# Two transformer layers on one core: the second layer's queries, keys and values with two token blocks sharing one pass of 64 + 64 inner rows

## The chip, the cores and the metric

The kernel runs on one core of a Trainium2 chip. The metric is the time of one execution in microseconds (us) on the device. Five engines work side by side: TensorE (PE in the profile; its weight loads are PEld), VectorE (DVE), ScalarE (ACT), GpSimd (POOL) and SyncE (SP), which here only issues transfers. TensorE writes its sums into banks of PSUM; the other engines take them out from there.

## The reference

Two equal layers over 2048 tokens of 576 features. Each is a sliding, dilated attention (32 heads of 18 features, 8 keys at distances 0, 2, .. 14) and a feed-forward part with SiLU, both on the normalized input, both added to it.

```python
def _A_ref(x, wqkv, wo):
    qkv = (x @ wqkv).reshape(B, S, 3, H, Dh).transpose(2, 0, 3, 1, 4)
    q, k, v = qkv[0], qkv[1], qkv[2]
    idx = pos[:, None] - (jnp.arange(8) * 2)[None, :]
    ...
    attn = _softmax(jnp.where(mask, logits, -1e9) * ...)
    return einsum("bhsw,bhswd->bhsd", attn, vg).reshape(B, S, D) @ wo

def _B_ref(x, w1, w2):
    return _silu(x @ w1) @ w2

for _ in range(2):
    x = x + _A_ref(_layernorm(x), A_wqkv, A_wo)
    x = x + _B_ref(_layernorm(x), B_w1, B_w2)
```

The change concerns `x @ wqkv` of the second layer alone: 576 inner features, 1728 columns.

## The kernel before

**Numbers.** Inputs are float32. A factor is split into two half-precision parts, high and low, and a product is made as high x high + high x low + low x high. For `x @ wqkv`, `passes` (a generator) lists the passes of TensorE: for each of the four full slices of 128 features three passes, and for the last 64 features two. Those two use a fifth slice of the input in which rows 0 to 63 hold the high parts of the 64 features and rows 64 to 127 their low parts. Slice 4 of the weights holds the high parts twice, slice 9 the low parts twice, so the first pass gives (high + low) x high, and the second (high + low) x low. That makes 14 passes of 128 rows and 128 tokens by 432 columns for a block.

**Tiles and stages.** The tokens are cut into four chunks of 512, a chunk into four blocks `j` of 128. A stage `s` from 0 to 7 is one chunk in one layer, so the second layer has the stages 4 to 7, and its first chunk is the fifth stage. The attention works in four units `u` of 8 heads; a unit's weights give 144 queries, keys and values each, 432 columns. In the second layer `attention` makes, for every stage, unit and block, one operation of 14 passes (`qkv_matmul`, line 726) into a bank of tag `zq`, and ScalarE takes it out into `kvs` and `qts` (lines 794 and 796). Then VectorE makes the products with the keys, the softmax and the sums over the values (lines 828 to 869).

The input's parts come from `layer_norm`: statistics (548), a Newton iteration for the reciprocal root (521 to 530), the normalized row (574), then the two halves (`halves`, 579, and `halves_lo`, 483), which go through a transposing transfer into tile `xa`. For the stages 6 and 7 the halves are made earlier, at the end of stages 2 and 3 (tile `xn`, `keep`), and loaded back.

The feed-forward part of the stages from 2 on (`ffn_pairs`) forms seven combinations of the input (`forms`, lines 1139 to 1182, tiles `yo`, `yh`, then `xb`) and multiplies each with a combination of the weights: a product is seven passes of 256 columns (line 1209). VectorE and ScalarE add them up (1213, 1216), apply SiLU, and split the result into the parts of `h` (1244, 1247), from which the second product is made, 12 passes of 288 columns at a time (line 1326). A pair of feature blocks `q` takes three banks in turn (tag `zz`).

**What sets the order.** Nothing is ordered by hand. Every operation is recorded with an engine, a duration that somebody wrote down, the tiles it reads and writes, and a priority; `Plan.order` plays the work through with these numbers and starts on each engine the ready operation of lowest priority number for which the tile slots are free. The order that comes out is the program. The tags `zz` and `zq` stand for the same four banks, so an operation that wants a bank competes with the feed-forward products. Attention operations of the second layer have priorities 3.0 to 3.4 on TensorE (`AT`), the feed-forward part of stage 3 has 3.5 and above, that of stage 4 has 4.5 and above: the second layer's attention is interleaved with the feed-forward work of the stages before it.

`S.slots("z", ...)`, `"misc"`, `"zz"` and `"zq"` all name the banks `z0`, `z1`, `misc0`, `misc1`; in the profile a product into one of them reads `z` or `misc`.

Of the kernel before, what the change touches and what calls it, by code (L numbers as in the profile page):

```python
# [14 lines left out]
ALU = mybir.AluOpType  # L15
AX = mybir.AxisListType

P = 128
D = 576
# [6 lines left out]
NC = 4  # L26
NJ = 4
# [248 lines left out]
def sliding_attention_silu_ffn(ctx: ExitStack, tc: tile.TileContext, x, wqkv, wo, w1, w2, out):  # L276
# [209 lines left out]

    def transposed(src, dst, key, j, prio, on_pe=False):


        if on_pe:  # L490
            m = Buf("acc")

            def turn():
                t = fl(T(m).bitcast(F16))
                for k in range(9):
                    nc.tensor.transpose(t[:, k * P:(k + 1) * P], T(src)[:, k, :], ident)
            op("PE", 0.5, turn, [(src, 0), (src, 1)], [m], prio)
            return op("ACT", 1.05, lambda: nc.scalar.activation(  # L498
                dst(), fl(T(m).bitcast(F16))[:, 0:9 * P].rearrange("p (a b) -> p a b", a=9), AF.Copy), [m], [(key, j)], prio - 9)
        return op("SP", 1.34, lambda: nc.sync.dma_start_transpose(dst(), fl(T(src))), [(src, 0), (src, 1)], [(key, j)], prio,  # L500
                  nbytes=P * 9 * P * 4)
# [32 lines left out]
    def layer_norm(xs, prio, into, on_act, on_pe=False, late=(), own=False, keep=None):  # L534
# [33 lines left out]
        for j in range(NJ):  # L568
# [8 lines left out]
            def halves(y=y, yh=yh):  # L577
                f = fl(T(yh))
                nc.vector.tensor_scalar(f[:, 0:D], T(y), 1.0, None, op0=ALU.mult)
                halves_lo(T(y), f, 1.0)  # L580
# [8 lines left out]
            else:  # L589
                op("DVE", 0.52, norm, [xs[j], (mv, j), (nt, "r", j)], [y] if keep else [y, (xT, "hold")], prio, after=late)  # L590
                o = op("DVE", 1.23, halves, [y], [(yh, 0), (yh, 1)], prio)
# [135 lines left out]

    def stage(g):
        t = T(g)
        return t[:, :QR] if g.tag == "hs" else fl(t.bitcast(F32))[:, :QR]  # L730
# [26 lines left out]
    def attention(s, xT, wq, more=None):  # L757
# [4 lines left out]
        for u in range(NU):  # L762
# [12 lines left out]
            else:  # L775
# [6 lines left out]
                else:  # L782
# [5 lines left out]
                    op("SP", 0.8, edge, [("eds", lay, par, u)], [(kv, "edge")], pr_, nbytes=20000, lanes=2, after=free)  # L788
                for j in range(NJ):
                    m = Buf("zq" if lay else "misc")  # L790
# [6 lines left out]
                    for a, b in ((0, 6), (6, 12), (12, 14)) if s + u + j == 0 else ((0, 14),):  # L797
                        op("PE", 2.56 * (b - a) / 14, lambda j=j, m=m, w=w, a=a, b=b: qkv_matmul(xT, w, j, m, a, b),
                           [(xT, j)] + [w.keys[5 * h + k] for k in range(a // 3, (b + 2) // 3) for h in range(2)],
                           [m, (kv, "hold")] if lay else [m], pr_, after=free)  # L800
# [672 lines left out]
    def norm(s):  # L1473
# [14 lines left out]
        normed[s] = layer_norm(xs, p, "xa", False, late=late, own=True)  # L1488
# [23 lines left out]
    for s in range(NL * NC):  # L1512
# [10 lines left out]
        if 2 <= s < NC:  # L1523
            layer_norm(X[s], AN[s + NC] + 0.0, None, False, own=True, keep=xn[s - 2])
# [46 lines left out]
```

## Time and profile before

| | us |
|---|---|
| median of 3 runs | 2135.34 (2133.32 to 2140.86) |
| the profiled execution | 2134.51 |
| its span in the profile | 2132.7 |
| TensorE's second-layer queries, keys, values | from 894 to 1497 of the span |

The profile is one execution. Its page gives each engine's busy time, and the trace behind it can be asked for a timeline, for the busy time in a stretch, and for one line of the program. In a timeline a row merges neighbours of one kind: `x14` is fourteen passes, the second column is the time from the start of the first to the end of the last. A pass's own duration includes the time to run through the array, so that passes overlap; the time that a pass takes up is the distance between two starts. A bracket at a row's end is idle time of the engine before it and what ended it.

### The profile page before, as it was taken

Reading aid. Unit: us, or ns where it says so; the run is one execution under the profiler, and the core shown is the slowest. Engines: PE = TensorE matmul, PEld = TensorE weight load, DVE = VectorE, ACT = ScalarE, POOL = GpSimd, SP = SyncE. Lnnn points to the kernel's source line nnn. Section 1 sums busy time; section 2 is a strip of 40 time slices with the busy share of each in tenths; the row PEclk is TensorE's granted clock in tenths of the full one; section 3 lists DMA queues with packets and bytes.
Section 4 is the critical chain, followed back from the end, with each engine's and each line's share of the span. In section 5 each row is a group of like instructions: output and inputs, shape, how many; then the busy total and the mean of one; then the engine's idle time right before and its main releaser. Section 6 shows DMA issues by size and latency. Waiting matters only on the chain.

```text
span 2132.7 us, 41915 instructions
## 1 busy us (share of the span) xinstructions
PE 2093.9 (98%) x16017; PEld 1554.6 (73%) x16017; DVE 1811.8 (85%) x2909; ACT 1025.3 (48%) x1857; POOL 388.7 (18%) x628
## 2 busy tenths in 40 slices
PE   9999899999999999999999999999999999999998
PEld 5556466656666788877777777777788888888887
DVE  8999999999977899789989998998997748666665
ACT  7555787644335455243424433333444444444442
POOL 2223656242232241011101010000000000000000
PEclk9999999999999999999999999999999999999999
DMA  6586777597889988795768996776999998779772
GB/s 183 155 228 247 246 261 249 189 258 254 253 170 283 302 248 255 169 263 169 211 179 211 227 300 187 192 194 192 262 302 308 335 262 227 225 208 274 214 209 69
DMA packets 377633, 489.08 MB, mean 229 GB/s; under 512 B 150600, under 2 KB 300724, under 8 KB 373080
## 3 DMA queue, kind: packets, MB, share of 16 engines
q1 hardware_dynamic: 332456, 336.85, 56.2%
q0 software_dynamic: 42960, 148.45, 21.6%
q8 instruction: 125, 2.05, 0.4%
q10 hardware_dynamic: 2016, 1.11, 0.2%
q14 instruction: 76, 0.62, 0.1%
HBM read 350.96 MB, written 86.85 MB: 205 GB/s over the span
## 4 chain that ended last, share of the span: by engine, by line
PE 62%; DMA 7%; DVE 5%; issue 3%; POOL 0%; ACT 0%; SPq 0%; DVEq 0%; POOLq 0%; ACTq 0%
PE acc L1326 17%; PE z L1209 12%; PE misc L1209 11%; PE acc L1299 9%; PE z L726 3%; PE acc L904 3%; PE misc L726 3%; PE acc L1387 3%; PE z L1368 2%; DMA w<-wfs 2%; DMA w<-w2s 1%; DMA wq<-in_B_w_dram 1%; DMA xb<-yo 1%; DVE prs L828 1%; DVE lg L832 1%
## 5 line engine op out<-in xcount | busy, mean ns | idle before, releaser
L1209 PEld LDWEIGHTS <-w 128*128 128x128 f16 x5292 | 516.7, 98 | 82.4 <-issue 8.9
L1326 PE MATMUL acc<-w,h 128*128 128x288 f16 x3456 | 448.7, 287 | 1.4 <-DVE h L1247 0.9
L1326 PEld LDWEIGHTS <-h 128*128 128x128 f16 x3456 | 338.3, 98 | 86.4 <-DVE h L1247 1.8
L1209 PE MATMUL z<-xb,w 128*128 128x256 f16 x2695 | 341.7, 273 | 3.9 <-DVE wq L1216 1.9
L1209 PE MATMUL misc<-xb,w 128*128 128x256 f16 x2597 | 331.5, 273 | 5.4 <-DMA w<-wfs 3.0
L1387 PE MATMUL acc<-w,h 128*128 128x288 f16 x1728 | 215.4, 286 | 1.1 <-DMA w<-w2s 1.1
L726 PEld LDWEIGHTS <-xa 128*128 128x128 f16 x1344 | 130.8, 98 | 111.9 <-issue 1.9
L1387 PEld LDWEIGHTS <-h 128*128 128x128 f16 x1728 | 168.3, 98 | 45.6 <-issue 1.5
L861 DVE TENSOR_TENSOR prs<-kvs,pe 128x1152 f32<-128x1152 f32 x128 | 169.8, 1350 | 0.8
L828 DVE TENSOR_TENSOR prs<-qts,kvs 128x2304 f32<-128x2304 f32 x64 | 163.3, 2552 | 5.4 <-DMA kvs<-kvs 2.8
L832 DVE TENSOR_REDUCE lg<-prs 128x128 f32<-128x2304 f32 x64 | 162.9, 2545 | 0.8
L915 DVE SCALAR_TENSOR_TENSOR x<-acc,d,x 128x576 f32<-128x576 f32 x136 | 110.1, 811 | 41.8 <-PE acc L1326 35.2
L1368 PE MATMUL z<-xb,w 128*128 128x512 f16 x588 | 130.9, 383 | 7.9 <-ACT h L1370 4.0
L868 DVE TENSOR_TENSOR prs<-prs 128x1152 f32<-128x1152 f32 (+1 forms) x128 | 135.0, 1055 | 3.3
L1308 DVE SCALAR_TENSOR_TENSOR x<-acc,d2x,x 128x576 f32<-128x576 f32 (+1 forms) x85 | 68.8, 810 | 68.5 <-PE acc L1299 68.4
L726 PE MATMUL z<-wq,xa 128*128 128x432 f16 x658 | 125.2, 346 | 0.0
L904 PE MATMUL acc<-wos,yo 128*128 128x288 f16 x896 | 113.7, 286 | 3.0 <-DMA yo<-yh 1.8
L1368 PEld LDWEIGHTS <-w 128*128 128x128 f16 x588 | 57.6, 98 | 78.1 <-issue 6.5
L1299 PEld LDWEIGHTS <-h 128*128 128x128 f16 x924 | 90.2, 98 | 24.0 <-DVE h L1271 2.6
L904 PEld LDWEIGHTS <-yo 128*128 128x128 f16 x896 | 87.4, 98 | 27.1 <-DMA yo<-yh 2.3
L726 PE MATMUL misc<-wq,xa 128*128 128x432 f16 x518 | 100.1, 346 | 2.7 <-ACT xa L498 1.3
L1368 PE MATMUL z<-xb,wq 128*128 128x512 f16 x420 | 94.5, 384 | 2.6 <-ACT h L1370 2.6
(300 smaller groups left out, 3158.9 us busy)
## 6 DMA issues: line engine op xcount, KB each, us to landing
w<-wfs SPq DMA_DIRECT2D x756, 160.0 KB, 3.9
w<-w2s SPq DMA_DIRECT2D x180, 288.0 KB, 4.8
wq<-wqs SPq DMA_DIRECT2D x17, 1080.0 KB, 6.1
kvs<-kd POOLq DMA_DIRECT2D x8, 1584.0 KB, 8.2
kvs<-wts SPq DMA_DIRECT2D x81, 144.0 KB, 2.7
w<-w1s SPq DMA_DIRECT2D x36, 320.0 KB, 9.2
wfs<-xa POOLq DMA_DIRECT2D x18, 640.0 KB, 4.9
w2s<-w POOLq DMA_DIRECT2D x36, 288.0 KB, 4.2
```

Of the source, the lines that this page charges most:

```text
L726: nc.tensor.matmul(T(m)[:, :3 * UC], a, b, start=n == 0, stop=n == len(pl) - 1)
L828: nc.vector.tensor_tensor(T(pr), T(qt)[:, j:j + 2, None, :].to_broadcast([P, 2, W, UC]), win(T(kv), j, 2), op=ALU.mult)
L832: nc.vector.tensor_reduce(T(lg)[:, j:j + 2].rearrange("p a w h -> p (a w h)"), T(pr).rearrange("p a w (h d) -> p (a w h) d", d=DH), axis=A ...
L861: nc.vector.tensor_tensor(T(pr)[:, a].rearrange("p w (h d) -> p w h d", d=DH), v, T(pe)[:, j + a, :, :, None].to_broadcast([P, W, UH, DH]) ...
L868: nc.vector.tensor_tensor(t[:, :, 0:h, :], t[:, :, 0:h, :], t[:, :, h:2 * h, :], op=ALU.add)
L904: nc.tensor.matmul(T(acc)[:, h, 0:288], a, b[:, h * 288:(h + 1) * 288], start=n == 0, stop=n == len(pl) - 1)
L915: nc.vector.scalar_tensor_tensor(t, acc[:, :, 0:288], d, t, op0=ALU.mult, op1=ALU.add)
L1209: nc.tensor.matmul(t, w[:, u, :], v[:, r, :], start=first and m == 0, stop=m == 6, skip_group_check=True)
L1299: nc.tensor.matmul(T(acc)[:, j, 0:KH], T(hb[t])[:, a, row[k], j * P:(j + 1) * P], T(wb[k, t])[:, w, :], start=k in (5, 1, 2) and t == 0 an ...
L1326: nc.tensor.matmul(T(acc)[:, h, 0:288], T(hb[t])[:, a, f, j * P:(j + 1) * P], T(wbs[t][f])[:, h, w, :], start=t == 0 and f == 0 and m == 0 ...
L1368: nc.tensor.matmul(T(z), v, u, start=m == 0, stop=m == len(pl) - 1)
L1387: nc.tensor.matmul(T(acc)[:, h, 0:288], T(hb[q])[:, a, j * P:(j + 1) * P], T(wbs[q][0])[:, h, w, :], start=q == 0 and m == 0, stop=q == n ...
```

## The change

Two blocks `j` and `j + 1` of a unit make a pair. Each keeps the first 13 of its 14 passes. The fourteenth, (high + low) x low, is reduced to high x low over 64 rows: the even block's on rows 0 to 63, the odd block's on rows 64 to 127, as two instructions of 64 rows each that write to different banks. (The term low x low of these 64 features is thereby left out.) For the odd block the high parts have to lie in rows 64 to 127, so its last slice holds the halves in swapped order, which the new `halves_turned` writes; the weights' slice 9 holds the low parts in both halves already, and for the 13 other passes the order of the two halves does not matter, since slice 4 of the weights holds the same rows twice.

The recorded operations are still one for each block. The even block's has its 13 passes and both half passes; it now takes both banks of the pair and reads both blocks of `xa`. The odd block's has 13 passes. Their written durations are 2.56 and 2.38, where both had 2.56.

```diff
+    def halves_turned(src, f):
+        nc.vector.tensor_scalar(f[:, 0:512], src[:, 0:512], 1.0, None, op0=ALU.mult)
+        nc.vector.tensor_scalar(f[:, D:D + 64], src[:, 512:D], 1.0, None, op0=ALU.mult)
+        for o, a, b, h in ((640, 0, 512, 0), (512, 512, D, D)):
+            nc.vector.scalar_tensor_tensor(f[:, o:o + b - a], src[:, a:b], 1.0, f[:, h:h + b - a],
+                                           op0=ALU.mult, op1=ALU.subtract)
...
-            def halves(y=y, yh=yh):
+            def halves(j=j, y=y, yh=yh):
                 f = fl(T(yh))
+                if swap and j % 2:
+                    halves_turned(T(y), f)
+                    return
                 nc.vector.tensor_scalar(f[:, 0:D], T(y), 1.0, None, op0=ALU.mult)
                 halves_lo(T(y), f, 1.0)
...
-                o = op("DVE", 1.23, halves, [y], [(yh, 0), (yh, 1)], prio)
+                o = op("DVE", 1.38 if swap and j % 2 else 1.23, halves, [y], [(yh, 0), (yh, 1)], prio)
...
+    def qkv_pair(xT, w, j, a, b, second):
+        xk = lambda i: lambda k: T(xT)[:, k, (j + i) * P:(j + i + 1) * P]
+        if second:
+            pl = list(passes(xk(1), w))[:13]
+            for n, (u, v) in enumerate(pl):
+                nc.tensor.matmul(T(b)[:, :3 * UC], u, v, start=False, stop=n == len(pl) - 1)
+            return
+        for n, (u, v) in enumerate(list(passes(xk(0), w))[:13]):
+            nc.tensor.matmul(T(a)[:, :3 * UC], u, v, start=n == 0, stop=False)
+        for i, m in ((0, a), (1, b)):
+            r = slice(64 * i, 64 * i + 64)
+            nc.tensor.matmul(T(m)[:, :3 * UC], xk(i)(4)[r], w(9)[r], start=i == 1, stop=i == 0)
...
+                pairs = [Buf("zq") for _ in range(NJ)] if lay else []
                 for j in range(NJ):
-                    m = Buf("zq" if lay else "misc")
+                    m = pairs[j] if lay else Buf("misc")
...
+                    if lay:
+                        op("PE", 2.56 if j % 2 == 0 else 2.38, lambda j=j, w=w, pairs=pairs: qkv_pair(
+                            xT, w, j - j % 2, *pairs[j - j % 2:j - j % 2 + 2], j % 2),
+                           [(xT, i) for i in ((j, j + 1) if j % 2 == 0 else (j,))] + w.keys,
+                           [m, pairs[j + 1], (kv, "hold")] if j % 2 == 0 else [m], pr_, after=free)
-                    for a, b in ((0, 6), (6, 12), (12, 14)) if s + u + j == 0 else ((0, 14),):
+                    for a, b in () if lay else ((0, 6), (6, 12), (12, 14)) if s + u + j == 0 else ((0, 14),):
...
-        normed[s] = layer_norm(xs, p, "xa", False, late=late, own=True)
+        normed[s] = layer_norm(xs, p, "xa", False, late=late, own=True, swap=True)
...
-            layer_norm(X[s], AN[s + NC] + 0.0, None, False, own=True, keep=xn[s - 2])
+            layer_norm(X[s], AN[s + NC] + 0.0, None, False, own=True, keep=xn[s - 2], swap=True)
```

Since the order is worked out from durations and free slots, it changes from the fifth stage's second unit to the end of the second layer's attention. Two places show what moved.

The first is on TensorE, the third block of the seventh stage's first unit. Before, its last passes into one bank stand ahead of the last group of second products (`w`, `h`) of the fourth stage:

```order
L726 LDWEIGHTS xa
L726 MATMUL misc_96<-wq,xa 128x432
L726 LDWEIGHTS xa
L726 MATMUL misc_96<-wq,xa 128x432
L1326 LDWEIGHTS h
L1326 MATMUL acc_99<-w_87,h 128x288
L1326 LDWEIGHTS h
L1326 MATMUL acc_99<-w_87,h 128x288
```

Now the same block ends in the two half passes (line 749), the second into the partner's bank, and the partner's 13 passes (line 743) follow at once:

```order
L746 LDWEIGHTS xa
L746 MATMUL z_94<-wq,xa 128x432
L749 LDWEIGHTS xa
L749 MATMUL z_94<-wq,xa 128x432
L749 LDWEIGHTS xa
L749 MATMUL misc_96<-wq,xa 128x432
L743 LDWEIGHTS xa
L743 MATMUL misc_96<-wq,xa 128x432
L743 LDWEIGHTS xa
L743 MATMUL misc_96<-wq,xa 128x432
```

Behind the partner's last pass stands the fifth stage's feed-forward part (products of `xb` and `w`):

```order
L743 LDWEIGHTS xa
L743 MATMUL misc_96<-wq,xa 128x432
L1238 LDWEIGHTS w_70
L1238 MATMUL z_95<-xb,w_70 128x256
L1238 LDWEIGHTS w_70
L1238 MATMUL z_95<-xb,w_70 128x256
```

The block has moved from ahead of the last second products of the fourth stage to behind the first two groups of second products of the fifth; its partner has hardly moved. Ahead of those groups two products of seven passes have come in its stead.

The second place is on VectorE, ahead of its first write of `h` in the fifth stage (line 1247, now 1276). `x_75` and `x_76` are the halves of the fourth stage's chunk, which is normalized here for the eighth stage. Before:

```order
L1216 TENSOR_TENSOR wq<-misc_97,wq 128x256
L574 TENSOR_SCALAR x_75<-x_75,mv_91,nt_92 128x576
L579 TENSOR_SCALAR yh<-x_75 128x576
L483 SCALAR_TENSOR_TENSOR yh<-x_75,yh 128x512
L483 SCALAR_TENSOR_TENSOR yh<-x_75,yh 128x64
L1216 TENSOR_TENSOR wq<-misc_96,wq 128x256
L1216 TENSOR_TENSOR wq<-z_95,wq 128x256
L574 TENSOR_SCALAR x_75<-x_75,mv_91,nt_92 128x576
L1247 SCALAR_TENSOR_TENSOR h<-h,sh_304 128x1024
L574 TENSOR_SCALAR x_76<-x_76,mv_91,nt_92 128x576 x2
```

and now:

```order
L1245 TENSOR_TENSOR wq<-misc_96,wq 128x256
L1245 TENSOR_TENSOR wq<-z_95,wq 128x256
L861 TENSOR_REDUCE lg_80<-prs 128x128
L488 TENSOR_SCALAR yh<-x_75 128x512
L489 TENSOR_SCALAR yh<-x_75 128x64
L491 SCALAR_TENSOR_TENSOR yh<-x_75,yh 128x512
L491 SCALAR_TENSOR_TENSOR yh<-x_75,yh 128x64
L869 TENSOR_TENSOR lg_80<-lg_80,mrow 128x256
L870 TENSOR_REDUCE mx_83<-lg_80 128x32
L871 TENSOR_TENSOR lg_80<-lg_80,mx_83 128x256
L1276 SCALAR_TENSOR_TENSOR h<-h,sh_304 128x1024
```

The odd block's halves (488 to 491) and both norms of `x_76` have come ahead of that write. The attention's product, sum and first softmax step (861 to 871 here) stood ahead of it before too, only further up; no row that stood ahead stands behind now.

More of the change, by code (lines that the diff above doesn't have):

```diff
@@ L532, in newton, with layer_norm @@
             nc.vector.tensor_scalar(T(nt)[:, 2, js], T(mv)[:, js, 0], -1.0, None, op0=ALU.mult)
-    def layer_norm(xs, prio, into, on_act, on_pe=False, late=(), own=False, keep=None):
+    def layer_norm(xs, prio, into, on_act, on_pe=False, late=(), own=False, keep=None, swap=False):
         st, mv, nt, xT = Buf("st"), Buf("mv"), Buf("nt"), Buf(into) if into else None
@@ L796, in evac @@
                         nc.scalar.activation(T(qt)[:, j, :], T(m)[:, 0:UC], AF.Copy, scale=d)
-                    for a, b in ((0, 6), (6, 12), (12, 14)) if s + u + j == 0 else ((0, 14),):
+                    if lay:
[4 more added lines that the diff above has]
+                    for a, b in () if lay else ((0, 6), (6, 12), (12, 14)) if s + u + j == 0 else ((0, 14),):
                         op("PE", 2.56 * (b - a) / 14, lambda j=j, m=m, w=w, a=a, b=b: qkv_matmul(xT, w, j, m, a, b),
                            [(xT, j)] + [w.keys[5 * h + k] for k in range(a // 3, (b + 2) // 3) for h in range(2)],
-                           [m, (kv, "hold")] if lay else [m], pr_, after=free)
+                           [m], pr_, after=free)
                     op("ACT", 0.78, evac, [m, ("su", u)], [(kv, j), (qt, j)], pr_ - (0 if s else 9))
```

## The prediction

> **What bounds the kernel now.** I read the head of the page first, then the engines' busy time in the stretch in which the second layer's queries, keys and values are made, then the timelines of TensorE and VectorE at one place in it.
>
> ```profile
> span 2132.7 us, 41915 instructions
> PE 2093.9 (98%) x16017; PEld 1554.6 (73%) x16017; DVE 1811.8 (85%) x2909; ACT 1025.3 (48%) x1857; POOL 388.7 (18%) x628
> 900.00:1500.00 600.00, 595.55 (x4599) 448.91 (x4598) 542.53 (x767) 238.71 (x467) 66.86 (x113) 1.00 0.77 210
> 894.00:1497.00 603.00, 168.12 (x896) 87.54 (x896) 1.00 0.77 209
> ```
>
> The third row gives, from 900 to 1500 us, the busy time of PE, PEld, DVE, ACT and POOL, then granted clock, DMA share and GB/s; the fourth is PE and PEld for line 726 alone. PE is busy for 595.55 of 600 us at full clock, so work taken off PE is worth its full length unless PE then waits for something else. That something is near: DVE is busy for 542.53 of the same 600. The 896 passes of line 726 are 64 blocks of 14: the change makes 32 pairs of them.
>
> The place to watch is the seam at which TensorE goes from the fourth chunk's feed-forward part to the fifth's, whose inputs VectorE has to make first. PE there (start, length, what, and in brackets the idle time before it):
>
> ```profile
> 1200.11 2.72 PE L726 MATMUL z<-wq,xa 128*128 128x432 f16 x14
> 1202.66 1.63 PE L1326 MATMUL acc<-w,h 128*128 128x288 f16 x12
> ...
> 1209.39 2.73 PE L726 MATMUL misc<-wq,xa 128*128 128x432 f16 x14
> 1211.95 1.27 PE L1326 MATMUL acc<-w,h 128*128 128x288 f16 x9
> ...
> 1220.78 0.93 PE L1209 MATMUL z<-xb,w 128*128 128x256 f16 x7
> 1221.54 0.93 PE L1209 MATMUL misc<-xb,w 128*128 128x256 f16 x7
> ...
> 1224.54 0.92 PE L1209 MATMUL z<-xb,w 128*128 128x256 f16 x7 [0.28 <-DVE h L1216]
> ...
> 1231.44 0.93 PE L1209 MATMUL z<-xb,w 128*128 128x256 f16 x7 [1.22 <-DVE wq L1216]
> 1232.20 0.65 PE L1326 MATMUL acc<-w,h 128*128 128x288 f16 x4
> 1233.12 2.62 PE L1326 MATMUL acc<-w,h 128*128 128x288 f16 x20 [0.27 <-DVE h L1247]
> 1235.58 2.72 PE L726 MATMUL z<-wq,xa 128*128 128x432 f16 x14
> ```
>
> The reader is to see three things. A block of 14 passes takes 2.55 us from its start to that of the next work (1200.11 to 1202.66): 182 ns a pass. A product of seven takes 0.76 us (1220.78 to 1221.54). And each wait at the seam names DVE. VectorE at the same place:
>
> ```profile
> 1216.30:1239.40 23.10, 22.02 (x56) 1.00 1.07 306
> 1216.37 0.43 DVE L1177 TENSOR_TENSOR yo<-wos,yo 128x256 f16<-128x256 f32 x1 [3.04 <-ACT yo L1172]
> ...
> 1228.79 0.57 DVE L574 TENSOR_SCALAR x<-x,mv,nt 128x576 f32<-128x576 f32 x1
> 1229.40 0.46 DVE L579 TENSOR_SCALAR yh<-x 128x576 f16<-128x576 f32 x1
> 1229.89 0.83 DVE L483 SCALAR_TENSOR_TENSOR yh<-x,yh 128x512 f16<-128x512 f32 x2
> ...
> 1231.79 1.28 DVE L1247 SCALAR_TENSOR_TENSOR h<-h,sh 128x1024 f16<-128x1024 f32 x1
> 1232.98 1.06 DVE L574 TENSOR_SCALAR x<-x,mv,nt 128x576 f32<-128x576 f32 x2
> ```
>
> DVE is busy for 22.02 of 23.10 us (first row), and at 1231.79 it writes the h for which PE waits at 1233.12. Here DVE sets the time, and PE only has to be there.
>
> **The change part by part.** *The passes.* A pair had 28 passes and now has 26 full ones and two of 64 rows. Side by side the two cost one pass, so 182 ns a pair are saved: 32 x 0.182 = 5.8 us, of which 17 pairs (3.1 us) stand ahead of the product at 1221.54 and 15 (2.7 us) behind. The trace has no pass of fewer than 128 rows (all read 128\*128), so the price is bounded from both sides:
>
> ```profile
> L726 PE MATMUL z<-wq,xa x658: 343/346/347, 151.3 to 1492.0; 128*128 128x432 f16 x165
> L726 PEld LDWEIGHTS <-xa x1344: 95/98/100, 17.1 to 1494.3; 128*128 128x128 f16 x192
> ```
>
> Below: 182 ns saved a pair. Above: if the array has to run empty before and after, each of two passages costs what a pass lasts beyond its slot, 346 - 182 = 164 ns, so 2 x 164 - 182 = 146 ns are lost a pair, and with two weight loads of 98 ns uncovered 342 ns. I take the saving: the nearest rows are the changes from 432 to 288 or 256 columns above, with another operand on either side, and they follow one another without a gap.
>
> *A rule to weigh.* After those rows: the Trainium skill, page "TensorEngine Tiling (Array Packing)", section Tiling Modes, states that a change of the tiling mode drains TensorE; its page "TensorE: Matmul & The Clock Gate", Part 3, has passes in separate row groups start about 4 ns apart. By the first alone the pair's sum would be nearer the upper bound, by the second it is the lower; no run here yet shows either.
>
> *The moved block.* The third block of the seventh chunk's first unit (1209.39 above) stood ahead of the seam. As it now needs two of the four banks at once, it stands behind the fifth chunk's first two groups of line 1326, next to its partner (1235.58). So PE comes to the product at 1221.54, for which it has the same work ahead otherwise, 2.55 + 3.1 = 5.6 us earlier. Work that stood ahead of the group at 1232.20 and is now behind it: 2.55 us, less two products of 0.76 us that went the other way: **+1.0 us**.
>
> *VectorE.* An odd block's halves take four instructions instead of three; the added one has 64 columns, and the copy loses 64 of 576.
>
> ```profile
> L483 DVE SCALAR_TENSOR_TENSOR yh<-x,yh 128x64 f16<-128x64 f32 x12 | 2.6, 218 | 0.0
> ```
>
> At most 0.22 us, less 64/576 of 0.46 us: 0.17 us a block, eight blocks. Seven are hidden in the 57 us that DVE is idle between 900 and 1500. At the seam the order matters more: ahead of that h stand two norms more (1.06 us, row 1232.98) and an odd block's halves (0.46 + 0.83 + 0.17 = 1.46 us), and nothing that stood ahead has left: **+2.5 us**. From below, the wait of 3.04 us at 1216.37 could swallow all of it, so 0; from above, a wait of that size more, 5.5 us. I take 2.5, since the added rows stand behind the place of that wait. Behind this h are queued the softmax and the next values of the attention, and PE's group at 1232.20.
>
> So the wait at the seam grows by 2.5 us (h later) and by 5.6 - 2 x 0.76 = 4.1 us (PE earlier): 6.6 us. The 5.8 us saved are more than spent, though part of that wait is the moved block's own time, which PE still does behind it.
>
> *The clock.* A wait can cost more than its length:
>
> ```profile
> 719.62 0.94 PE L1209 MATMUL z<-xb,w 128*128 128x256 f16 x7 [0.60 <-DMA w<-wfs]
> 722.25 1.33 PE L1209 MATMUL misc<-xb,w 128*128 128x256 f16 x7 [1.69 <-DMA w<-wfs]
> 722.80:726.20 3.40, 3.40 (x17) 0.52 0.96 299
> ```
>
> After 2.3 us of waiting the clock was 0.52 for 3.4 us, some 1.6 us lost. At 1222 to 1233 it stayed at 1.00 with waits spread out. Bounds 0 and 1.6; I take half, **+0.8 us**.
>
> *At nothing:* the banks (the second is taken 2.4 us sooner; three others turn meanwhile, and if they didn't, a wait as at 1231.44, 1.22 us, is the price); the even block's wait for its partner's transposed block (made well before, except for the first pair); weight loads that change places on SP, where PE waited this much from 900 to 1850:
>
> ```profile
> PE misc L1209 <- DMA w<-wfs: 1.3, 2, 0.8
> ```
>
> Their price, if the cover goes, is another 1.3 us. The few stores that swap neighbours on POOL release nothing PE waits for soon.
>
> *Sum*, from the group at 1232.20 on, since what happens before it ends in the wait: +2.5 + 1.0 - 2.7 + 0.8 = +1.6 us. The profiled execution took 2134.51 us (span and 1.8 us around it): 2136.1. The median shown, 2135.34, lies 0.83 above it: **2137 us**.
>
> **The rivals.**
> *The saving passes through.* If VectorE makes the seam's inputs as early as PE now comes, all 5.8 us remain: 2129.5. For it: PE's own waits at the seam are short now. Against it: 22.02 of 23.10 us, and more DVE work ahead, not less.
> *The halves don't run side by side* (the change doesn't do what it says): 28 slots as before, and only the order is left: 2.5 + 1.0 = +3.5, with little clock loss 2139.
> *The array runs empty at each change of rows*, the case on the slower side. Place: both sides of each pair's half passes; price 146 ns a pair. The 17 pairs ahead (2.5 us) fill the time that the moved block left, so the wait hides them; behind come 15 x 0.146 = 2.2: 2.5 + 1.0 + 2.2 = +5.7, 2141. With the loads uncovered, 342 ns, the 17 pairs (5.8 us) exceed the 2.55 us by 3.3, which then replaces the 2.5: 3.3 + 1.0 + 15 x 0.342 = +9.4, 2144.7. It is slower by over 0.3% from 3.5 + 15c = 6.4, c = 0.19 us a pair. The Trainium skill's rule on draining ("TensorEngine Tiling (Array Packing)", Tiling Modes) would lead to this case.
>
> **How the numbers follow.** A difference under 0.3% (6.4 us) is about what a measurement of this kernel can't tell from no change. Chances: my sum 0.42, passing through 0.10, no side by side 0.15, running empty 0.33, of which 0.13 with c above 0.19. Faster by over 0.3% needs more than the whole saving, below 2128.9: 0.03. Slower, above 2141.7: 0.13. Within: 0.84. The range goes from the saving passing through nearly whole, 2130, to running empty with half of the loads uncovered, 2143.
>
> **What would show it.** The two half passes' starts lie a few ns apart (right) or 182 ns (no side by side); the gap from the last full pass to the first half, and from the second half to the next full pass, is 182 ns, or near 346 (running empty). The group that stood at 1232.20 waits for DVE's h, and PE's waits at the seam add up to some 8 us instead of the 1.8 in the brackets above. If those waits stay as they are, the seam was judged wrongly; if new waits of over 2 us appear elsewhere, the order was.

## The result and the profile after

| | median of the runs, us | span of the profiled execution, us |
|---|---|---|
| before | 2135.38 (2133.32 to 2140.86, 7 runs) | 2132.7 |
| after | 2147.51 (2139.32 to 2150.63, 7 runs) | 2148.9 |

After against before is 1.005 (95%: 1.0033 to 1.0066): some 12 us slower by the medians, 7 to 14 by the interval, outside the forecast range of 2130 to 2143. Three executions, two of the kernel before at 4473 and 5892 us and one with two shared passes at 9103 us, were in a slow state and are left out here and below. The profiled execution of the changed kernel is the slowest of its seven runs, 16.1 us above that of before.

The head of its page, engines' busy time:

```profile
span 2148.9 us, 41911 instructions
PE 2098.4 (98%) x16017; PEld 1551.2 (72%) x16017; DVE 1814.0 (84%) x2917; ACT 1025.5 (48%) x1857; POOL 388.3 (18%) x628
```

PE is busy for 4.5 us more, and the span grew by 16.2: most of it is waiting. The half passes first, by line (count, then min/median/max of the duration in ns), and then one pair on the timelines of PE and of its weight loads:

```profile
L749 PEld LDWEIGHTS <-xa x64: 91/93/93, 900.7 to 1502.8; 64*128 64x128 f16 x64
L749 PE MATMUL misc<-wq,xa x32: 352/353/354, 900.7 to 1502.8; 64*128 64x432 f16 x32
```

```profile
1143.72 2.54 PE L746 MATMUL misc<-wq,xa 128*128 128x432 f16 x13
1146.19 0.36 PE L749 MATMUL misc<-wq,xa 64*128 64x432 f16 x2
1146.47 2.55 PE L743 MATMUL misc<-wq,xa 128*128 128x432 f16 x13
1148.86 1.44 PE L746 MATMUL z<-wq,xa 128*128 128x432 f16 x7
```

```profile
1146.18 0.10 PEld L749 LDWEIGHTS <-xa 64*128 64x128 f16 x2 [0.36 <-issue]
1146.47 2.12 PEld L743 LDWEIGHTS <-xa 128*128 128x128 f16 x13 [0.19 <-issue]
```

Both half passes of a pair together span 0.36 us, one alone lasts 0.353: they run side by side, 3 ns apart in their starts. But thirteen passes at 182 ns would bring the half passes at 1146.09, and they start at 1146.19; and the next full pass comes 0.28 us behind them instead of 0.18. Over all 32 pairs the last full pass and the first half pass start 278 ns apart, the second half pass and the next full pass 285, and the full pass after that follows 194 ns later instead of 182. A pair takes 5.14 us (1143.72 to 1148.86); 28 full passes take 5.11 (1143.94 to 1149.05 in the kernel with the order alone, below).

Within a block a weight load starts 2 ns after the pass before its own. Here the load of the half pass starts at 1146.183 us, 275 ns after the last full pass (1145.908) and 93 ns after that pass's slot is over; the load of the next full pass is late in the same way. A load takes 91 to 99 ns, about what each change costs.

PE at the seam, to be laid beside the rows of before in the prediction:

```profile
1205.75 2.61 PE L1355 MATMUL acc<-w,h 128*128 128x288 f16 x20
1208.20 2.54 PE L746 MATMUL z<-wq,xa 128*128 128x432 f16 x13
...
1213.34 6.04 PE L1355 MATMUL acc<-w,h 128*128 128x288 f16 x48
1219.22 0.93 PE L1238 MATMUL z<-xb,w 128*128 128x256 f16 x7
1219.98 0.93 PE L1238 MATMUL misc<-xb,w 128*128 128x256 f16 x7
1224.67 1.68 PE L1238 MATMUL z<-xb,w 128*128 128x256 f16 x7 [3.77 <-DMA xb<-yo]
1226.14 1.70 PE L1238 MATMUL misc<-xb,w 128*128 128x256 f16 x7
...
1233.79 0.92 PE L1238 MATMUL z<-xb,w 128*128 128x256 f16 x7 [0.26 <-DVE wq L1245]
...
1238.76 0.66 PE L1355 MATMUL acc<-w,h 128*128 128x288 f16 x4 [0.98 <-ACT h L1273]
1240.75 1.15 PE L1355 MATMUL acc<-w,h 128*128 128x288 f16 x8 [1.33 <-DVE h L1276]
...
1245.90 0.27 PE L1238 MATMUL misc<-xb,w 128*128 128x256 f16 x1 [0.95 <-DVE wq L1245]
```

The brackets add up to 7.29 us. Behind the first wait seven passes take 1.47 us (1224.67 to 1226.14) instead of 0.76: half the clock, for 35 passes. Then VectorE, in the two stretches up to the first write of `h` (its start ends the second stretch; the columns are length, busy time and number, granted clock, DMA share, GB/s), of before:

```profile
900.00:1195.00 295.00, 267.33 (x398) 1.00 0.75 206
1195.00:1231.79 36.79, 32.87 (x69) 1.00 1.04 252
```

and of after:

```profile
900.00:1195.00 295.00, 261.33 (x394) 1.00 0.73 200
1195.00:1239.41 44.41, 41.61 (x81) 0.92 1.05 292
```

`h` comes 7.62 us later. Of this 2.74 us are more work (302.94 against 300.20) and 4.88 are more idle time (36.47 against 31.59): 6.00 more ahead of 1195, of which 1.12 are made up behind. The largest waits of VectorE for PE between 900 and 1195 (us in total, how many, the longest), of before:

```profile
DVE x L915 <- PE acc L1326: 6.9, 6, 1.8
DVE o L915 <- PE acc L904: 2.9, 1, 2.9
```

and of after:

```profile
DVE x L944 <- PE acc L1355: 7.4, 9, 1.6
DVE o L944 <- PE acc L933: 4.4, 1, 4.4
```

With the smaller ones, the waits for PE there grew from 11.7 to 16.0 us and those for ScalarE from 2.8 to 4.8.

Where PE loses is worked out by counting columns: the time at which the same number of columns has been issued in one execution and in that of before. The changed kernel is 1.9 us late at 1215, 8.8 at 1260, 10.8 at 1500, 12.7 at 1565, 15.8 at 1765 and 16.1 at the end. The same kernel again, the first of the experiments, has 1.9, 9.6, 10.4, 11.1, 12.0 and 11.6: the 7 to 8 us at the seam are always there, while the 2 and 3 us of 1540 and 1770 vary from execution to execution.

### The profile page after: what moved, and what is told of

It is laid out like the page before. It is cut to its first block, busy times and chain, and to the rows that moved or that the text cites. A ratio compares the mean times of both kernels' runs of the same rounds, so it can differ in the third digit from the quotient of the medians.

```text
span 2148.9 us, 41911 instructions
## 1 busy us (share of the span) xinstructions
PE 2098.4 (98%) x16017; PEld 1551.2 (72%) x16017; DVE 1814.0 (84%) x2917; ACT 1025.5 (48%) x1857; POOL 388.3 (18%) x628
## 4 chain that ended last, share of the span: by engine, by line
PE 80%; DMA 9%; DVE 7%; issue 2%; ACT 1%; SPq 1%; POOL 0%; DVEq 0%; ACTq 0%; POOLq 0%
PE acc L1355 18%; PE z L1238 12%; PE misc L1238 11%; PE acc L1328 8%; PE z L1397 7%; PE acc L1416 7%; PE z L736 5%; PE acc L933 5%; PE misc L743 2%; PE z L743 2%; PE misc L746 2%; PE z L746 2%; DMA wq<-in_B_w_dram 1%; DMA w<-w2s 1%; DMA xb<-yh 1%
## 5 line engine op out<-in xcount | busy, mean ns | idle before, releaser
L1399 ACT ACTIVATE h<-z,d 128x512 f32<-128x512 f32 x72 | 49.1, 682 | 83.9 <-PE z L1397 80.7
L1242 ACT ACTIVATE wq<-misc 128x256 f32<-128x256 f32 x97 | 36.8, 380 | 94.9 <-PE misc L1238 94.9
L1328 PE MATMUL acc<-kvs,h 128*128 128x288 f16 x498 | 76.2, 286 | 0.4 <-DVE h L1300 0.4
```

The costliest lines, as they stand in the source:

```text
L1328: nc.tensor.matmul(T(acc)[:, j, 0:KH], T(hb[t])[:, a, row[k], j * P:(j + 1) * P], T(wb[k, t])[:, w, :], start=k in (5, 1, 2) and t == 0 an ...
```

## The experiments

Each was timed against the kernel before on the same chip. "Late" is PE's lateness by columns, as above.

### Order or half passes

> The changed kernel unaltered, for a second profile beside the others on one chip. Theory A (the two half passes start together but each change between 128 and 64 rows costs some 98 ns, so a pair takes 19 ns more than 28 full passes, and the loss is the new order's waits): some 10 us over the kernel before, with the wait at the seam near 1225 us of the same size again (3.8 us, and a half clock after it), and the waits near 945, 957, 1550 and 1780 us only if they belong to the order. Theory B (the pairs themselves cost the time, by waits inside them): the same total, but the pairs' gaps differ from those of the first profile.

2147.72 (2144.16 to 2151.53), ratio 1.0053 (1.0037 to 1.0070).

The new order with 28 full passes a pair:

```diff
-        for n, (u, v) in enumerate(list(passes(xk(0), w))[:13]):
-            nc.tensor.matmul(T(a)[:, :3 * UC], u, v, start=n == 0, stop=False)
-        for i, m in ((0, a), (1, b)):
-            r = slice(64 * i, 64 * i + 64)
-            nc.tensor.matmul(T(m)[:, :3 * UC], xk(i)(4)[r], w(9)[r], start=i == 1, stop=i == 0)
+        pl = list(passes(lambda k: T(xT)[:, k, (j + i) * P:(j + i + 1) * P], w))
+        for n, (u, v) in enumerate(pl):
+            nc.tensor.matmul(T(m)[:, :3 * UC], u, v, start=n == 0, stop=n == len(pl) - 1)
```

> The changed kernel's order, banks and swapped halves with 14 full passes of 128 rows in every block (28 a pair, no half pass). Theory A: as the changed kernel, 0.6 us less of passes, so some 9 to 10 us over the kernel before, and the same wait at the seam near 1225 us. Theory B: the loss goes with the half passes, so within 3 us of the kernel before.

2145.87 (2142.74 to 2151.97), ratio 1.0045 (1.0028 to 1.0062); 7.8 us lost at the seam. And the half passes in the order of before, in the 22 pairs that stand together there (these blocks have the swapped halves too):

> The kernel before with its own order; swapped halves for the odd blocks, and 22 of the 32 pairs (those whose odd block follows the even one directly on TensorE) with the two half passes, put at the start of the odd block's passes; the other 10 pairs keep 28 full passes. Theory A: 22 x 0.019 = +0.4 us and little else, so within 2 us of the kernel before. Theory B: 22/32 of the loss, some +8 us. If the half passes saved what they were meant to, 22 x 0.182 = -4.0 us.

2135.68 (2132.07 to 2140.41), ratio 0.9998 (0.9987 to 1.0010). The order alone carries the loss; the half passes alone neither save nor cost, to within 3 us.

### The price of a change of rows

A full pass between the two half passes, so four changes a pair:

```diff
-            nc.tensor.matmul(T(m)[:, :3 * UC], xk(i)(4)[r], w(9)[r], start=i == 1, stop=i == 0)
+            nc.tensor.matmul(T(m)[:, :3 * UC], xk(i)(4)[r], w(9)[r], start=i == 1, stop=False)
+            if i == 0:
+                u, v = pl[12]
+                nc.tensor.matmul(T(a)[:, :3 * UC], u, v, start=False, stop=True)
```

> The changed kernel with the even block's last full pass put between the two half passes: four changes of rows a pair instead of two, and the halves no longer together. Theory A: 2 x 98 + 182 - 3 = 375 ns a pair more, 32 x 0.375 = +12 us over the changed kernel, less what falls into the seam's wait (17 pairs ahead of it): +6 to +12 us. If the price is not one of the change but of the pair as such, +182 ns a pair, +3 to +6 us.

2157.80 (2156.34 to 2160.16), ratio 1.0101 (1.0084 to 1.0118): 10 us above the changed kernel. Over the 64 changes in either direction the starts are 278 or 289 ns apart on the way to 64 rows (the first and the second half pass) and 286 on the way back. Then the other way round, two shared passes for one pair of changes:

```diff
+        for n, k in enumerate((9, 4)):
+            for i, m in ((0, a), (1, b)):
+                r = slice(64 * i, 64 * i + 64)
+                nc.tensor.matmul(T(m)[:, :3 * UC], xk(i)(4)[r], w(k)[r], start=i == 1 and n == 0, stop=i == 0 and n == 1)
```

> The changed kernel with a second shared pass for each pair: of the last 64 features only high x high and high x low are made, each as two half passes side by side (24 full and 4 half passes a pair; low x high of these 64 features is left out), with the order of the changed kernel. It tells what the two stalls of about 100 ns a pair belong to. Theory A: to the change of rows. Then the second pair of half passes starts 182 ns after the first, a pair takes 0.18 us less than in the changed kernel, 5.8 us of TensorE over all 32. Rival B: to every half pass, whose weight load is not drawn ahead. Then the second pair of half passes starts some 280 ns after the first, and a pair takes 0.09 us less, 2.8 us over all. Of the time I expect 2.7 us less than the changed kernel under A (the 15 pairs behind the fifth stage's first products; those ahead end in the wait there), so near 2145, and near 2146.5 under B.

2140.94 (2134.98 to 2146.87), ratio 1.0025 (1.0007 to 1.0044). PE of this kernel in one pair:

```profile
1147.11 2.35 PE L746 MATMUL z<-wq,xa 128*128 128x432 f16 x12
1149.39 0.35 PE L750 MATMUL z<-wq,xa 64*128 64x432 f16 x1
1149.40 0.35 PE L750 MATMUL misc<-wq,xa 64*128 64x432 f16 x1
1149.59 0.34 PE L750 MATMUL z<-wq,xa 64*128 64x432 f16 x1
1149.59 0.34 PE L750 MATMUL misc<-wq,xa 64*128 64x432 f16 x1
1149.87 0.36 PE L743 MATMUL misc<-wq,xa 128*128 128x432 f16 x1
```

The second shared pass follows after 0.19 us, a plain slot; the 0.28 us stand only where the number of rows changes. So the price belongs to the change (theory A). The time is some 6 us below that of the changed kernel, where I expected 2.7. The two intervals leave this difference open by 5 us either way, but the lateness by columns says the same: 5.1 us at 1260 against 8.8 and 9.6, with 17 pairs (3.1 us) made until then. So what is saved ahead of the seam seems to count too. The same in the order of before:

> The kernel with the pairs in the order of before (22 of the 32 pairs), with a second shared pass as in the other run (low x high of the last 64 features is left out in these pairs). It tells whether time taken off TensorE in the old order reaches the end. The changes of rows are the same 44, but 22 slots of 182 ns go, 4.0 us of TensorE. If TensorE sets the end all through, the time falls by 4.0 us, to some 2131.7. If VectorE sets it at the fifth stage's first products, what is saved ahead of them ends in a wait there, and only the pairs behind count: some 1 to 2 us, near 2134.

2132.95 (2126.92 to 2138.71), ratio 0.9983 (0.9968 to 0.9998): 3.7 us by the medians (0.4 to 6.8 by the interval), near the 4.0 taken off PE. Time saved on PE does reach the end in that order, though the interval doesn't tell all of it from a part.

### Which part of the recording makes the order

The first two have 28 full passes a pair and one of two recorded changes alone: the claim of two banks (and of both blocks of `xa`), or the shorter duration of the odd block on PE. The longer duration of an odd block's halves on VectorE is in neither.

> 28 full passes a pair and swapped halves; of what the planner is told, only the even block's claim of both banks (and both input blocks) is kept, written durations are those of the kernel before. The third block of the seventh stage's first unit stands behind the seam here too. If the claim of two banks makes the costly order: +6 to +12 us over the kernel before, most of it at the seam near 1225 us. If the written durations do: within 2 us.

2152.66 (2145.58 to 2156.48), ratio 1.0060 (1.0036 to 1.0084).

> 28 full passes a pair and swapped halves; the planner is told the odd block's shorter duration (2.38 for 2.56) and nothing else, each block claims its own bank. The block stands ahead of the seam as in the kernel before. If the claim of two banks makes the costly order: within 2.5 us of the kernel before. If the written durations do: +6 to +12 us.

2144.65 (2137.63 to 2151.66), ratio 1.0023 (1.0006 to 1.0040). By the ratios the claim is the larger part, though the intervals touch, and the other order lost something too. Next the claim everywhere except in the seventh stage's first unit, and in that unit alone (there the block stands behind the seam); the diff is of the second:

```diff
-                           [m, pairs[j + 1], (kv, "hold")] if j % 2 == 0 else [m], pr_, after=free)
+                           ([m, pairs[j + 1], (kv, "hold")] if j % 2 == 0 else [m]) if (s == 6 and u == 0) else [m, (kv, "hold")], pr_, after=free)
```

> As the run with the order alone (28 full passes, two banks claimed, shorter written durations), except for the seventh stage's first unit, whose blocks claim one bank each; its third block then stands ahead of the seam. Theory C (the moved block makes the seam's wait): within 4 us of the kernel before, no wait of over 2 us near 1225 us. Theory D (blocks that stand together ahead of the seam make VectorE wait for TensorE, some 5 us up to 1195 us, and so make the seam's inputs late): +6 to +10 us with the wait at the seam still there.

2142.66 (2136.31 to 2147.62), ratio 1.0013 (0.9997 to 1.0029); 1.7 us lost at the seam, and in the profiled execution 6 more behind 1500.

> 28 full passes a pair and swapped halves; two banks claimed and shorter durations written in the seventh stage's first unit alone, whose third block then stands behind the seam. Theory C: +6 to +9 us, the wait at the seam there. Theory D: within 4 us, since VectorE's idle time up to 1195 us stays as in the kernel before (some 22 us from 900 us on).

2144.19 (2139.63 to 2149.10), ratio 1.0033 (1.0019 to 1.0046); 1.7 us at the seam, more behind it. VectorE up to `h` in this kernel:

```profile
900.00:1195.00 295.00, 265.68 (x401) 1.00 0.76 203
1195.00:1233.13 38.13, 35.71 (x72) 1.00 1.03 269
```

Its idle time up to `h` is 31.74 us, as before the change (31.59): the added idle time comes from the claim in the other units. The other kernels say the same: 41.43 us with the claim alone and 35.40 with the claim except in one unit, 31.99 with the durations alone. The moved block alone, or the late VectorE alone, costs 1.7 us at the seam; together they cost 5.6 (the claim alone) to 7.8. Each of these kernels has an order of its own, so this is no clean sum of two causes.

### Taking the seam apart

The rest of the runs keep the order of the changed kernel and take one thing out of it. In four of them one sum of VectorE, or two, is replaced by a short copy, so that these do not compute the same. The first two:

> The changed kernel with one sum of VectorE taken out: the reduction of 2.55 us at 1213.97 (one unit, two blocks) is replaced by a copy of 128 columns, about 0.2 us, so that these logits are not the sums over the 18 features; order and all else stay. It stands on VectorE two steps ahead of the form (1217.16) for whose transfer TensorE waits 3.77 us at 1224.67. Theory D, VectorE being late at the seam is the cause: the form is 2.35 us earlier, that wait falls to some 1.4 us, too short for the half clock (2.7 us), and TensorE behind the seam is some 5 us less late than in the changed kernel, near 2142.5. Rival E, the wait only moves on to the next h: 2.35 us less, near 2145. Rival C, the transfers or TensorE's own early arrival set it: the wait stays, 2147.5.

2145.66 (2144.01 to 2150.71), ratio 1.0048 (1.0030 to 1.0067). The wait stayed at 3.80 us.

> As the other run, and the same unit's second reduction (2.55 us at 1234.32, ahead of the first write of h) replaced by such a copy too. Theory D: the first write of h comes another 2.35 us earlier, the waits ahead of it (0.98 and 1.33 us at 1238.76 and 1240.75) go, and another 2 us of lateness with them, near 2140.5. Under E all of the second 2.35 us counts as well, near 2143. Under C it stays near the other run.

2147.02 (2141.59 to 2152.12), ratio 1.0055 (1.0035 to 1.0074). Theory D's numbers did not come: in the second kernel VectorE now waits for PE (0.81 and 2.19 us for line 1361, the second products), and the form, though written earlier, is not sent earlier. What holds it is SP's queue, here of the changed kernel:

```profile
1214.05 4.21 SPq L954 DMA_DIRECT2D w<-w2s  x5
1218.37 3.42 SPq L1211 DMA_TRANSPOSE xb<-yo  x2
1221.89 3.68 SPq L1211 DMA_TRANSPOSE xb<-yh  x2
```

Five loads of second weights, which wait for PE's second products to free their tiles, stand ahead of the transfers that PE waits for. Next they were put behind two of them:

```diff
+    loads, behind = on_sp[at[0]:at[0] + 5], on_sp[at[0] + 6]
+    ordered = [o for o in ordered if o not in loads]
+    n = ordered.index(behind) + 1
+    ordered[n:n] = loads
```

> The changed kernel, nothing left out, with one change of order on SP's queue: the five loads of second weights (w2s, 1214.05 to 1218.26), which stand there ahead of the two transfers of the form for which TensorE waits 3.77 us at 1224.67, stand behind them now. They are wanted by TensorE only at 1238.76. Theory F, the queue is the cause: the transfers are issued at some 1217.7, when the form is written, instead of 1218.37, and have no 1.44 MB ahead of them, so that they land after some 3.5 us (the median before) instead of 6.0. The wait falls from 3.77 to some 0.6 us, the half clock (2.7 us) does not come, and the time falls by about 5.8 us, to 2142. Theory D, VectorE is the cause (the form is written late): only the 0.7 us of the earlier issue is won, the half clock stays, and the time is near 2147.

2151.62 (2145.79 to 2155.42), ratio 1.0068 (1.0049 to 1.0086): not the 2142 of theory F. The wait at the third product fell to 2.08 us, and one of 4.51 came at the sixth.

> The swapped queue of the other run and the one sum less of an earlier run together (these logits are not the sums). That sum alone left the wait at 3.80 us: the form came 1.4 us earlier relative to TensorE and waited in the queue. Under F with VectorE next in line, the transfers now issue when the form is written, some 1.4 us earlier than in the other run: no wait is left at that product, and the time is near 2141 or 1 us below the other run. Under D this is the first kernel in which the form's earlier time can pass through: near 2144, 3 us below the other run.

2149.11 (2143.50 to 2152.60), ratio 1.0057 (1.0037 to 1.0077). PE of the second kernel:

```profile
1218.29 0.93 PE L1244 MATMUL z<-xb,w 128*128 128x256 f16 x7
1219.05 0.93 PE L1244 MATMUL misc<-xb,w 128*128 128x256 f16 x7
1219.82 0.93 PE L1244 MATMUL z<-xb,w 128*128 128x256 f16 x7
...
1228.21 3.17 PE L1244 MATMUL misc<-xb,w 128*128 128x256 f16 x14 [5.93 <-DMA xb<-yh]
```

The wait at the third product is gone, so queue and VectorE had held that transfer together; it has moved to the sixth, whose transfers now stand behind the loads. With all four ahead of them (`at[0] + 8`):

> As the kernel with the swapped queue, nothing left out, but all four transfers of the forms stand ahead of the five loads of second weights on SP's queue. With two ahead, the wait at the third product fell from 3.77 to 2.08 us without half clock, and a wait of 4.51 us came at the sixth, for the two transfers left behind the loads. Theory F: the wait at the third product stays near 2.1 (the form itself is written late there), that at the sixth falls to 1 us at most, no half clock comes, and what TensorE loses between 1210 and 1245 falls from some 8 us in the changed kernel to 4 to 5: near 2144. If the loads, now some 5 us later, are what TensorE waits for next (rival G), a wait of 2 us or more for w2s comes near 1240 and the time stays near 2147.

2146.29 (2142.63 to 2153.84), ratio 1.0047 (1.0031 to 1.0063). PE:

```profile
1223.05 0.94 PE L1238 MATMUL z<-xb,w 128*128 128x256 f16 x7 [1.89 <-DMA xb<-yo]
...
1228.76 0.92 PE L1238 MATMUL misc<-xb,w 128*128 128x256 f16 x7 [2.48 <-ACT wq L1242]
...
1233.48 0.94 PE L1238 MATMUL z<-xb,w 128*128 128x256 f16 x7 [1.48 <-DMA w<-wfs]
```

and the windows view of the same kernel (PE, PEld, DVE, ACT, POOL, then the granted clock):

```profile
1220.00:1235.00 15.00, 9.15 (x81) 7.45 (x79) 14.41 (x39) 4.25 (x11) 1.08 (x2) 1.00 1.05 277
```

The long wait has fallen apart into three, for a transfer, a bank (ScalarE takes it out, line 1242) and a weight load; the clock stays at 1.00; and PE still loses 6.8 us. VectorE is busy for 14.41 of these 15 us.

> The same, and one sum of VectorE less as in the earlier runs (these logits are not the sums). With the queue swapped and the sum out, the wait at the third product was gone and 5.93 us came at the sixth, for the two transfers behind the loads. Theory F with VectorE next: no wait over 0.5 us is left at the products of the fifth stage's first forms, only those for h (some 1 and 2.5 us) remain, and TensorE loses 3 to 4 us between 1210 and 1245: near 2142. Rival G as in the other run: near 2146.

2147.88 (2141.78 to 2151.61), ratio 1.0052 (1.0034 to 1.0071): a wait of 4.41 us for a bank, 6.7 us lost. Neither theory's numbers held. Last, PE's own order (first line: the pair at 1208.20 and what ScalarE takes out of it, put behind the 48 passes at 1213.34), and in the second of the two runs VectorE's with it (second line: one unit's attention behind `h`); the numbers are those of recorded operations:

```diff
+    behind(3181, 3580, 3581, 3582, 3583)
+    behind(3763, 3531, 3532, 3533, 3534)
```

> The changed kernel, nothing left out, with one change of order: on TensorE the pair that starts at 1208.20 (28 slots, 5.1 us) stands behind the last four groups of second products of the fourth stage instead of ahead of them, just ahead of the first products of the fifth stage that wait; what ScalarE takes out of its banks stands behind the pair. VectorE and SP's queue keep their order. Theory C, the pair's place on TensorE is the cause: the groups come 5.1 us earlier, the loads that wait for them leave SP's queue earlier, VectorE's last sum of x and all behind it too, and the pair stands where TensorE waited: it loses 2 to 3 us at this place instead of 8, near 2142. Theory D, VectorE's late rows are the cause: its order is the same, so the awaited form comes at most 1 to 2 us earlier, TensorE loses 6 to 7 us, near 2146.

2147.52 (2139.93 to 2158.12), ratio 1.0044 (1.0028 to 1.0061): 8.5 us lost at the seam. Theory C, that the pair's place on PE is the cause, fell: it asked for 2 to 3. The 6 to 7 of theory D were exceeded, too.

> The same, and on VectorE one unit's product, sum and first softmax step (2.55, 2.54 and 1.42 us at 1230.86, 1234.32 and 1237.97), which in the kernel before stood ahead of its idle time at 1216.37, stand behind the two writes of h (1239.41). Theory D: h comes up to 5 us earlier than in the other run, TensorE's waits ahead of h (0.98 and 1.33 us) go and it loses 2 us less there than in the other run, if the attention that is now later is not awaited next; near 2140 to 2144. Theory C: h was late only because TensorE was; h comes earlier but TensorE gains under 1 us over the other run.

2149.15 (2147.21 to 2158.04), ratio 1.0062 (1.0042 to 1.0083): 13.6 us lost. VectorE of this kernel:

```profile
1235.54 0.43 DVE L488 TENSOR_SCALAR yh<-x 128x512 f16<-128x512 f32 x1 [5.07 <-DMA xn<-yh]
...
1236.74 1.28 DVE L1276 SCALAR_TENSOR_TENSOR h<-h,sh 128x1024 f16<-128x1024 f32 x1
```

With the attention out of the way, the odd block's halves, which now stand ahead of `h`, wait for the store of the halves before them, and `h` waits behind. This is one more chain that ends within a few us of the others; the attention's work had hidden it. Behind `h` PE then waits 3.44 us more for a bank (at 1246.60, named line 1242), with half clock before and after it, which is why it loses so much more than `h` is late.

How late `h` is, and how late PE is at 1260, each less PE's lateness at 1215 (us):

| kernel | h | PE |
|---|---|---|
| changed kernel, and again | 5.8, 6.2 | 7.0, 7.8 |
| order only; four changes | 6.3; 6.5 | 7.8; 7.2 |
| two shared passes | 5.7 | 5.7 |
| one sum less; two | 6.8; 5.4 | 7.0; 5.6 |
| queue swapped; with sum | 7.1; 7.9 | 8.9; 9.6 |
| all four ahead; with sum | 5.7; 6.5 | 6.8; 6.7 |
| pair behind groups; attention too | 6.7; 5.7 | 8.5; 13.6 |
| two banks alone; durations alone | 3.1; 3.0 | 5.6; 3.7 |
| claim except one unit; in one unit | 2.5; -0.3 | 1.7; 1.7 |
| pairs in old order; two shared there | -1.1; -0.2 | -1.3; -0.3 |

In all but two (two banks alone, attention too) PE leaves the seam as late as `h`, to within 2 us, whichever input it waits for on the way. This doesn't say which holds which, since `h` itself is made from PE's products. What brings the loss down is another order ahead of the seam; none of the links taken out here does. Which part of the order would have to go back is not settled by these runs: each link taken out uncovered another. None of the kernels that compute all that the changed one does beats the one before.

## Why the prediction was wrong, step by step

**The passes: the step "I take the saving" failed.** The half passes do run side by side, but each change of rows costs 96 ns on the way in (278 - 182) and 103 on the way out, and 12 more at the next pass (194 - 182): with 3 ns between the halves a pair takes 182 less and 214 more, +0.03 us, +1.0 us in all instead of -5.8. The place is that of the rival "running empty", both sides of the half passes, but not its price: some 100 ns a passage where I had put 164, so that its point, c = 0.19 us a pair, was far from reached. What the 100 ns are stays open. They are as long as one weight load, and two loads left uncovered, with no running empty, would give 2 x 98 - 182 = 14 ns a pair. But by the trace the lost time lies ahead of the late load, whose pass starts 4 ns after it. And this load starts 72 ns before the recorded end of the last full pass (1146.255, an end that the profile models), so the array had not run empty by that end either. No run separates the two. The nearest rows that I went by, changes from 432 to 288 columns, keep 128 rows and say nothing of this. The Trainium skill ("TensorEngine Tiling (Array Packing)", Tiling Modes) has a change of the tiling mode drain TensorE: the trace agrees in so far as each change costs some 100 ns. It also agrees with the Trainium skill's starts a few ns apart in separate row groups ("TensorE: Matmul & The Clock Gate", Part 3), 3 ns here. I had weighed the two rules as if one had to give way.

**What lies ahead of the seam: failed too.** I let 3.1 of the 5.8 us end in the wait for VectorE. The two shared passes speak against it: 5.8 us less on PE made the kernel some 6 us faster and PE 4 us less late at 1260. That fits a VectorE that itself waits for PE ahead of the seam (11.7 us of it between 900 and 1195 before the change).

**VectorE: the work right, the idle time missed.** `h` came 7.6 us later, where I had 2.5 and at most 5.5. The work ahead of it grew by 2.74 us, about as counted. The other 4.88 us are idle time: I took the 57 us that VectorE is idle as a reserve. But much of that idle time is waits for PE and ScalarE, and these grew. That the claim of two banks made them grow is shown: where it was left to one unit, the added idle time was gone and `h` came 1.3 us later. The way is argued: the claim makes the two blocks of a pair stand together, 5.1 us of PE in a row in which nothing is made that VectorE waits for.

**The moved block: agrees.** I had +1.0 us behind `h`; PE's lateness at 1260 exceeds that of `h` by 1.2 us (8.8 against 7.6). In the other kernels with the block behind the seam it is 0 to 2.5, and 7.9 in one, so that the good match may be luck.

**The clock: wrong in both ways.** The half clock cost 2.6 us (35 passes took 6.41 us from 1224.67 to 1231.08, at 0.76 for seven 3.80), not 0.8; but in the kernel with all four transfers ahead it did not come, and PE lost as much at the seam. There it seems to have lain within the wait for `h` and cost little of its own. Over the whole kernel it can count for more: see the last section.

**At nothing:** two of the three terms turned into waits. SP's order, together with VectorE, held the transfer of the 3.77 us; banks made 2.48 and 4.41 us once that was away. For the third, the even block's wait for its partner's block, no wait shows. I had asked for each what it cost alone; taken out one by one, each uncovered the next.

**What would show it.** I asked for some 8 us of waits at the seam: 7.3, but by luck. The time by which PE was to come earlier fell away (by columns it was 1.9 us late at 1215), `h` came 5.1 us later than forecast, and 3.77 of the 7.3 us stand at a transfer that the forecast doesn't have. New waits of over 2 us elsewhere were to show the order misjudged: 2.03 us at 1550 and 2.08 us at 1781 in the profiled execution, part of what varies between executions.

The sum with these sizes: 7.6 for `h` and 1.2 behind it, 8.8 at 1260, where I had 3.5 and 0.8 for the clock. Behind, 0.5 to 2 us until 1500, where I had -2.7, and 1 to 5 us at 1540 and 1770 with the new order there, where I had nothing: 10 to 16 us, and 12 by the medians. The largest step that failed is VectorE's +2.5. The order alone, with full passes, was 9.6 us slower (6 to 13).

## What to carry to other kernels

A pass of half the rows pays only if several stand between two changes of rows: here two changes cost a little more than one full pass of 432 columns, so one shared pass gained nothing and a second one gained its whole slot. In a plan where several engines feed each other with a few us to spare, a gain of 0.3% on one engine is of the size of what the new orders here lost (0.1 to 0.6%): change the instructions and keep the order, then look whether the time comes through. And idle time of an engine whose work is awaited is no reserve: ask what it waits for, and whether the change makes that later.

## What the runs showed of the hardware

The clock, over the 20 profiled executions behind their first 100 us (a wait taken here as the distance of two passes' starts less the slot of the first): of 35 waits of 3.0 us and more all were followed within 2 us by passes at half the clock, of 36 from 2.5 to 3.0 us 25, of 38 from 2.0 to 2.5 us 15, of 75 from 1.5 to 2.0 us 5. Most such stretches last 2.9 to 3.4 us and cost 1.4 to 1.7; behind waits of 3.9 us and more some last 4.7 to 5.9 and cost 2.3 to 2.9. The Trainium skill ("TensorE: Matmul & The Clock Gate", Part 1) has the clock halved after an idle window of some 3.4 us; here 2 to 3 us were enough in 40 of 74 cases. That it falls in one execution and not in the next is part of why executions of one kernel differ by several us: over some 280 executions, each compared with others of its kernel, one with a granted clock lower by 0.001 took 2.3 us longer (correlation -0.67), and 0.001 of 2140 us is 2.1 us by itself. The granted clock averages 0.996 in the changed kernel and 0.998 in the one before. By the same rate that is some 3 to 5 us of the 11 to 12, an estimate from above, since part of the half clock lies within waits, and the waits that bring it are the order's.
